# A Fourier mixing layer with a low-rank token mixer: where V, W1, W2 and the second batch are loaded

## The chip, the cores and the metric

The kernel runs on one core of a Trainium2 chip. The core has a matrix engine (TensorE, PE in the profile), a vector engine (VectorE, DVE), an activation engine (ScalarE, ACT), a general engine (GpSimd, POOL) and a queue engine that only issues transfers (SyncE, SP). Each engine works through its own instructions in order and waits for the others by semaphores. Transfers between the chip's memory and the on-chip buffers run on 16 DMA engines; they can be issued from SP (queue q1 in the profile), from ACT (q10) and from POOL (q0). The metric is the device time of one execution in microseconds (us); less is better. The time before is the median of three runs.

## The reference

The input `x` has 8 batches of 3136 tokens with 256 channels. A two-dimensional Fourier transform is taken over tokens and channels and its real part kept. To that a low-rank mixing of tokens is added, and then a channel MLP with a residual.

```python
X = np.fft.fft(np.fft.fft(x, axis=1), axis=2).real      # (8, 3136, 256)
h = X.transpose(0, 2, 1) @ U @ V                        # U (3136, 32), V (32, 3136)
u = X + h.transpose(0, 2, 1)
out = u + np.maximum(u @ w_ch1, 0.0) @ w_ch2            # (256, 1024), (1024, 256)
```

All arrays are float32.

## The kernel before

**Factoring of the transform.** 3136 is 49 times 64. Stage 1 transforms over one factor (`s1_single` for one batch, `s1_steps` for a pair), writes the result `z` to memory (`zturn`), and the *turn* (`turn`, L228) reads it back transposed as the coefficient tile `g`: 64 partitions, 25 blocks `k`, 256 channels, in runs of 512 bytes. Stage 3 (`s3_steps`, matmuls at L283) multiplies `g` with the table `T` and gives the tokens `q`. The lower half of `g`, partitions 64 to 127, holds the low-rank term: `te_single` (L256, one batch) or `te_steps` (L240, a pair) computes the projection of the signal on U; it is masked (`te_out`, L237) and copied into `g` 25 times (`spread`, L267). Half of `T` therefore holds V. The transform over channels is folded into the weights: stage 1's inputs are added and subtracted with their mirror images, and W1 is multiplied with a cosine and sine table `Q` before use (`W1p`, `W1m`). W2 is folded by an addition and a subtraction (`w2_fold`, L624).

**Order.** The order of instructions is written by hand. The *head* handles batch 0 alone, before any MLP work can start. In the code's order it issues the load of U on SP (L408) and batch 0's four x tiles on POOL (`load_single`, L107: a direct and a mirrored load each, cast from float32 to bf16), then on POOL V twice (L420 and L421, into partitions 64 to 95 and 96 to 127) and W1 (L423); builds tables on POOL, DVE and ACT; runs stage 1 in eight steps `s1b0[0]` to `s1b0[7]`, every second one storing to `zturn` (L222) from SP; and issues the turn (L569) on SP and ACT and W2's load (L572) on SP. POOL casts V into `T` (L582), ACT writes its mirrored part (L580), and after that come POOL's loads of batch 1 (L608, L609). TensorE then does `te_single` (L589), W1's product with `Q` (`w1ps`, L591 to L600, eight float32 matmuls) and the first stage-3 steps. `keep_warm(n)` (L437) issues n matmuls on zeros, so that TensorE isn't idle.

**The main loop.** For each pair of batches there are 13 chunks of up to 512 tokens, and for each chunk four steps: `mlp1` (L326) computes a quarter of the hidden layer of this chunk, `mlp2` (L338) a quarter of the outputs of the chunk before, which SP stores (L360, four stores every second step). `plan(p)` (L666) places all other work at these 52 steps of a pair: stage 3 of the current pair's second batch, and, by `place_next(nx, a, gap, s3lo)` (L675), the eight chunk loads of the next pair from step `a` on, `gap` steps apart, POOL's fold (L131) 3 steps behind each load, DVE's fold (L122 to L124) 6 behind, stage 1 (L172) 8 and 9 behind, the turn and the projection right after the last of them, and stage 3 from step `s3lo`. The pair 0 has batch 1 in addition: its stage 1 at steps 6 to 13, its turn at 15, `te_single` at 17, stage 3 at 20 to 31. Pair 1 is placed with `(9, 2.3, 43)`, pairs 2 and 3 with `(3, 2.3, 40)`. `load_uz` (L661, step 12) loads the projection's table `UZ` in two transfers of 1600 rows of 128 bytes.

Of the kernel before, what the change touches and what calls it, by code (L numbers as in the profile page):

```python
# [22 lines left out]
def kernel(  # L23
# [9 lines left out]
    nc = tc.nc  # L33
# [194 lines left out]
    def turn(pr, b, parts, engines=(nc.sync,)):  # L228
        g = gpool.tile([P, NK1, D], BF16, tag=f"g{b}", name="g")
        src = zd[pr.p % 2, b].rearrange("k cn d -> cn k d")  # L230
        for i, (k0, k1) in enumerate(parts):
            engines[i % len(engines)].dma_start(out=g[0:64, k0:k1], in_=src[:, k0:k1, :])
        pr.g[b] = g
# [22 lines left out]
    def te_single(pr, b, spread):  # L256

        ps = psd.tile([P, 2, D], FP32, tag="ps", name="teps")
        for k in range(NK1):
            nc.tensor.matmul(ps[0:64, 0, :], us[:, k], pr.g[b][0:64, k, :], start=(k == 0), stop=(k == NK1 - 1))  # L260
        te_out(pr, b, ps, slice(0, 64), spread)
# [153 lines left out]
    part[0][3] = load_single(0, 3)  # L415
    nc.gpsimd.memset(x32[0][:].bitcast(FP32), 0.0)
    part[0][0] = load_single(0, 0)
    kio_t = gpool.tile([P, NK1, D], BF16, tag="g0", name="kio")
    kio = kio_t[0:64].bitcast(I32).rearrange("p k (s j) -> p (k s) j", s=2)[:, 0:NK1, :]
    nc.gpsimd.dma_start(out=uv[64:96], in_=moe_V)  # L420
    nc.gpsimd.dma_start(out=uv[96:128], in_=moe_V)  # L421
    w1r = tmp([P, 2, H], "w1r", FP32R)
    nc.gpsimd.dma_start(out=w1r[:], in_=moe_w_ch1.rearrange("(h p) j -> p h j", p=P))  # L423

    nc.gpsimd.iota(kio, pattern=[[1, NK1], [N1, 64]], base=0, channel_multiplier=0)
    nc.gpsimd.iota(kio[32:33, 0:NK1:2], pattern=[[0, 13], [1, 64]], base=0, channel_multiplier=0)
# [8 lines left out]
    nc.vector.memset(idle.bitcast(FP32), 0.0)  # L435

    def keep_warm(n):  # L437
        ps = psh.tile([P, 2, 512], FP32, tag="h", name="warm")
        for i in range(n):
            nc.tensor.matmul(ps[:, 0], idle[:, 0:P], idle[:, P:640], start=True, stop=True)  # L440

    keep_warm(12)
    nc.vector.memset(pi[:], math.pi * (1.0 - 2.0 ** -21))
# [54 lines left out]
    ups_v = ups[0:64, :, 0:384].rearrange("p i (k r) -> p i k r", k=12)  # L498
    nc.scalar.copy(rv[:, :, :, 0, :], ups_v)
    ua = tmp([64, NK1, 64], "ua", FP16)  # L500
    A, V = copy_act, copy_dve
    s1b0 = list(s1_single(first, 0, part[0], [A, V, A, V, A, V, A, A],
                          lambda n: (nc.sync, nc.scalar if n == 7 else nc.sync)))
# [11 lines left out]
        ts(pv[:, 7 + i:8 + i], m[:], off, 192.0)  # L515
    s1b0[2]()
    s1b0[3]()
    keep_warm(3)
    for i in range(2):
        for t in range(3):  # L520
            ts(an2[:, i, t, :, i], jf[0:PR, 0:32], pv[:, 5 + i:6 + i], pv[:, 7 + t:8 + t])
    mask_bits(an2[:], 16)
    s1b0[4]()
    sin_of(Fs[:, 3:9], an2[:].rearrange("p a t k c -> p (a t) k c"), 16)
    s1b0[5]()


    pn = tmp([64, 2], "pn")
# [3 lines left out]
    nc.vector.memset(pn[32:33, 0:1], 0.5)  # L532
    nc.vector.memset(pn[32:33, 1:2], 32.25)
    ta2 = kio.bitcast(FP32)
    ts(ta2, kio, pn[:, 0:1], pn[:, 1:2])
    mask_bits(ta2, 18)

    for k0, k1 in [(0, 16), (16, 25)]:
        ps = psh.tile([P, 16, 64], FP32, tag="h", name="uups")
        for k in range(k0, k1):  # L540
            o = ps[0:64, k - k0]
            nc.tensor.matmul(o, ua[:, k], ub[:, k].unsqueeze(1).to_broadcast([64, 2, R]),
                             start=((k - k0) % 8 == 0), stop=True, skip_group_check=True)
            if k:
                mk = 24 - k
                nc.tensor.matmul(o, ua[:, k], rv[:, mk // 12, mk % 12].rearrange("p s r -> p (s r)"),
                                 start=False, stop=True, skip_group_check=True)
        (copy_dve if k0 else copy_act)(us[:, k0:k1], ps[0:64, 0:k1 - k0])
    keep_warm(2)
    s1b0[6]()  # L550
    s1b0[7]()
    sin_of(T[0:64, :, 0:64], ta2, 18)
    keep_warm(10)

    pl = tmp([P, 1], "pl")
    ts(pl[:], pf[:], 1.0 / D, None)
    jq = ypool.tile([P, 3, P], FP32, tag="y", name="jq")  # L560
    ts(jq[:, 0, 0:65], jf[:, 0:130:2], pl[:], 128.25)
    ts(jq[:, 0, 65:P], jf[:, 2:P:2], pl[:], 128.5)
    for i in range(2):
        ts(jq[:, 1 + i, 0:64], jf[:, 1:P:2], pl[:], 128.25 + 0.5 * i)
        ts(jq[:, 1 + i, 64:P], jf[:, 1:P:2], pl[:], 128.5 + 0.5 * i)
    mask_bits(jq[:], 16)
    Q = tmp([P, 3, P], "Q", FP32R)
    sin_of(Q[:], jq[:], 16)
    turn(first, 0, [(0, 8), (8, 16), (16, NK1)], [nc.sync, nc.scalar])  # L569
    g1 = gpool.tile([P, NK1, D], BF16, tag="g1", name="w2_f")  # L570
    w2_f = g1[:, 0:16].bitcast(FP32).rearrange("p (t s) d -> p t s d", s=2)
    nc.sync.dma_start(out=w2_f, in_=moe_w_ch2.rearrange("(t p) (s d) -> p t s d", p=P, s=2))  # L572
    nc.vector.tensor_copy(T[0:64, :, 64:128], T[0:64, :, 63::-1])
    sgv = tmp([P, 1], "sgv")
    ts(sgv[:], pf[:], 96.0, -2.0, AL.is_ge, AL.mult)
    ts(sgv[:], sgv[:], 1.0, None, AL.add)
    bp_sin = residual_tables()

    Vk = uv.rearrange("p (k2 k1) -> p k1 k2", k1=N1)
    nc.scalar.mul(T[64:128, 1:NK1, 64:128], Vk[64:128, 48:24:-1, :], sgv[64:128])  # L580
    for lo, hi in [(0, 9), (9, 17), (17, NK1)]:
        nc.gpsimd.tensor_copy(T[64:128, lo:hi, 0:64], Vk[64:128, lo:hi, :])  # L582
    held = []

    def spread_first(g, te):
# [5 lines left out]
    for c in range(2):  # L591
        cs = slice(c * 512, (c + 1) * 512)
        ps = psh.tile([P, 2, 512], FP32, tag="h", name="w1ps")
        for blk in range(2):
            for i in range(2):
                nc.tensor.matmul(ps[:, blk], Q[:, blk * (1 + i)], w1r[:, i, cs], start=(i == 0), stop=(i == 1))
        if c:
# [156 lines left out]
```

## Time and profile before

| What | us |
|---|---|
| median of three runs | 504.78 (502.74 to 511.37) |
| profiled execution, its own time | 506.79 |
| span of the profiled execution | 504.9 |
| first matmul on the first coefficients (L283) | 48.92 |
| first second-layer matmul (L345) | 58.65 |
| end of TensorE's work | about 496 |
| mean granted TensorE clock | 0.955 of full speed |

The span is the time between the first and the last instruction; the profiled execution took 1.9 us more than it, and 2.0 us more than the median. The page gives busy time and share of each engine, the span in 40 slices, the DMA queues, the chain of work that ended last, and the costliest groups of instructions. In the answers of the trace a row of a timeline gives the start, the duration, the engine, the source line, the operation with output and inputs, the shapes, the count, and in brackets how long the engine had been idle and what ended that. A row of a window gives each engine's busy time in it, then TensorE's granted clock, the busy share of the 16 DMA engines and the GB/s moved.

### The profile page before, as it was taken

Reading aid. Unit: us, or ns where it says so; the run is one execution under the profiler, and the core shown is the slowest. Engines: PE = TensorE matmul, PEld = TensorE weight load, DVE = VectorE, ACT = ScalarE, POOL = GpSimd, SP = SyncE. Lnnn points to the kernel's source line nnn. Section 1 sums busy time; section 2 is a strip of 40 time slices with the busy share of each in tenths; the row PEclk is TensorE's granted clock in tenths of the full one; section 3 lists DMA queues with packets and bytes.
Section 4 is the critical chain, followed back from the end, with each engine's and each line's share of the span. In section 5 each row is a group of like instructions: output and inputs, shape, how many; then the busy total and the mean of one; then the engine's idle time right before and its main releaser. Section 6 shows DMA issues by size and latency. Waiting matters only on the chain.

```text
span 504.9 us, 9394 instructions
## 1 busy us (share of the span) xinstructions
PE 446.6 (88%) x3624; PEld 319.3 (63%) x3684; DVE 221.3 (44%) x512; ACT 285.5 (57%) x387; POOL 138.8 (27%) x145
## 2 busy tenths in 40 slices
PE   6607899379999999998999999979999999999993
PEld 2405566256778677765777777756776777766772
DVE  7821642225752544757314535865225444221211
ACT  4421744316774655775655566768456655666660
POOL 7480032427513202655150005663130000000000
PEclk9965999859999999998999999999999999999998
DMA  9999047845747824885495226766582222222323
GB/s 131 199 164 176 3 116 211 207 98 169 212 132 163 181 64 133 223 261 167 133 160 169 50 69 194 227 215 187 139 153 60 64 65 69 68 74 69 89 53 75
DMA packets 69345, 68.03 MB, mean 135 GB/s; under 512 B 17412, under 2 KB 62284, under 8 KB 69236
## 3 DMA queue, kind: packets, MB, share of 16 engines
q1 hardware_dynamic: 53780, 44.93, 36.5%
q0 software_dynamic: 11536, 14.77, 14.3%
q10 hardware_dynamic: 3984, 7.73, 4.6%
q8 instruction: 29, 0.48, 0.4%
q14 instruction: 16, 0.13, 0.1%
HBM read 36.36 MB, written 34.28 MB: 140 GB/s over the span
## 4 chain that ended last, share of the span: by engine, by line
PE 71%; DVE 3%; DMA 3%; ACT 2%; issue 1%; SPq 1%; ACTq 0%; DVEq 0%
PE ops L345 30%; PE hps L334 28%; PE ops L348 4%; PE ps L283 3%; PE ps L172 2%; PE teps L248 2%; ACT hT L336 2%; DMA out_dram<-ob 2%; DMA g<-zturn 2%; DVE yb L124 1%; PE teps L260 1%; SPq L360 1%; DVE ob L355 1%; ACT om L354 1%; DVE yb L123 1%
## 5 line engine op out<-in xcount | busy, mean ns | idle before, releaser
L336 ACT ACTIVATE hT<-hps 128x1024 bf16<-128x1024 f32 (+1 forms) x208 | 202.4, 975 | 135.1 <-PE hps L334 121.9
L345 PE MATMUL ops<-W_91,hT 128*128 128x256 bf16 x1568 | 226.4, 274 | 0.5 <-DVE W_91 L625 0.3
L345 PEld LDWEIGHTS <-hT 128*128 128x128 bf16 x1568 | 146.0, 98 | 35.0 <-issue 0.3
L355 DVE TENSOR_TENSOR ob<-ops,om 128x256 f32<-128x256 f32 (+1 forms) x100 | 41.9, 419 | 203.3 <-ACT om L354 199.5
L334 PE MATMUL hps<-q,W1p 128*128 128x512 bf16 (+1 forms) x420 | 102.6, 355 | 3.3 <-DVE q L79 1.2
L334 PE MATMUL hps<-q,W1m 128*128 128x512 bf16 x354 | 96.9, 383 | 3.7 <-ACT hT L336 1.9
L131 POOL TENSOR_TENSOR y<-xa,xb 98x1020 f32<-98x1020 f32 (+1 forms) x24 | 55.0, 2293 | 125.8 <-DMA xa<-in_x_dram 95.9
L79 DVE CAST q<-ps 128x512 bf16<-128x512 f32 (+3 forms) x120 | 64.5, 559 | 25.5 <-PE ps L283 19.0
L334 PEld LDWEIGHTS <-W1p 128*128 128x128 bf16 x448 | 40.6, 98 | 28.3 <-issue 3.9
L76 ACT CAST z<-ps 128x512 bf16<-128x512 f32 x57 | 33.4, 586 | 39.2 <-PE ps L172 31.1
L334 PEld LDWEIGHTS <-W1m 128*128 128x128 bf16 x384 | 36.2, 99 | 29.2 <-issue 4.3
L348 PEld LDWEIGHTS <-q 128*128 128x128 bf16 x392 | 38.6, 98 | 21.6 <-issue 1.2
L354 ACT COPY om<-ops 128x256 f32<-128x256 f32 (+1 forms) x100 | 36.8, 368 | 9.9 <-PE ops L345 9.2
L356 DVE TENSOR_TENSOR ob<-ops,om 128x256 f32<-128x256 f32 (+1 forms) x100 | 40.9, 409 | 0.0
L283 PE MATMUL ps<-T,g 128*128 128x128 bf16 (+1 forms) x400 | 37.5, 219 | 1.5 <-DVE q L79 1.5
L348 PE MATMUL ops<-Bp,q 128*128 128x128 f16 x200 | 38.4, 219 | 0.0
L267 POOL COPY g<-te 64x1024 int32<-64x1024 int32 (+1 forms) x21 | 22.5, 1118 | 57.3 <-DVE te L237 31.8
L348 PE MATMUL ops<-Bm,q 128*128 128x128 f16 x192 | 37.3, 221 | 0.0
L260 PE MATMUL teps<-g,us 64*64 64x256 bf16 x50 | 11.0, 415 | 27.4 <-DMA g<-zturn 27.4
L283 PEld LDWEIGHTS <-g 128*128 128x128 bf16 x400 | 29.8, 99 | 6.8 <-issue 1.9
L102 POOL DMA_INDIRECT xb<-in_x_dram,idx x24 | 25.3, 1054 | 9.8 <-PE ps L216 5.2
L260 PEld LDWEIGHTS <-us 64*64 64x64 bf16 x50 | 8.3, 167 | 30.0 <-DMA g<-zturn 16.7
(129 smaller groups left out, 247.5 us busy)
## 6 DMA issues: line engine op xcount, KB each, us to landing
out_dram<-ob SPq DMA_DIRECT2D x392, 64.0 KB
xa<-in_x_dram SPq DMA_DIRECT2D x24, 392.0 KB
g<-zturn SPq DMA_DIRECT2D x7, 800.0 KB
zturn<-z ACTq DMA_DIRECT2D x9, 512.0 KB
xs<-in_x_dram POOLq DMA_DIRECT2D x16, 196.0 KB, 8.4
zturn<-z ACTq DMA_DIRECT2D x3, 448.0 KB
zturn<-z ACTq DMA_DIRECT2D x9, 128.0 KB
w1r<-in_moe_w_ch_dram POOLq DMA_DIRECT2D x1, 1024.0 KB, 15.0
```

Of the source, the lines that this page charges most:

```text
L76: nc.scalar.copy(o, i)
L79: nc.vector.tensor_copy(o, i)
L102: nc.gpsimd.indirect_dma_start(out=ck.xb.rearrange("p l d -> p (l d)"), out_offset=None, in_=x_g, in_offset=bass.IndirectOffsetOnAxis(ap=i ...
L131: nc.gpsimd.tensor_tensor(ck.y[:, 0:n, 1:256], ck.xa[:, 0:n, 1:256], rb[:, :, 255:0:-1], op=AL.add)
L283: nc.tensor.matmul(o, lt, r, start=st, stop=True, skip_group_check=True)
L334: nc.tensor.matmul(ps[:, i, 0:n], (W1p if ch.sg > 0 else W1m)[:, blk, j], q[:, blk, c0:c0 + n], start=(blk == 0), stop=(blk == 1))
L336: nc.scalar.activation(ch.h[:, 2 * jp:2 * jp + 2, 0:n], ps[:, :, 0:n], AF.Relu)
L345: nc.tensor.matmul(ps, ch.h[:, j, t * P:(t + 1) * P], W2[:, j, :], start=(j == 0 and t % 2 == 0), stop=(j == JT - 1), skip_group_check=True)
L348: nc.tensor.matmul(ps[:, j], q[:, j, tk], (Bp if ch.sg > 0 else Bm)[:, j], start=False, stop=False, skip_group_check=True)
L354: nc.scalar.copy(om[:, 0:n], ch.po[:, 0:n, 1])
L355: nc.vector.tensor_tensor(ob[:, 0:n, 0:P], ch.po[:, 0:n, 0], om[:, 0:n], op=AL.add)
L356: nc.vector.tensor_tensor(ob[:, 0:n, P:D], ch.po[:, 0:n, 0], om[:, 0:n], op=AL.subtract)
```

## The change

V is loaded once, on SP right after U. POOL casts it into `T` before its table work, and DVE copies the partitions 64 to 95 of `T` into 96 to 127. W1 is loaded on SP after the fourth stage-1 step; DVE adds and subtracts its halves, and `w1ps` becomes four matmuls. `w1ps` goes ahead of `te_single`, with eight warm matmuls before and after it. W2's load waits for batch 0's turn: a small copy on POOL reads all three parts of `g` and writes into W2's tile. The loads of batch 1, later on POOL, stand behind that copy. In the plan the stages have one more step between load and fold, and the placements of pair 0 and `place_next` get other numbers.

```diff
     nc.sync.dma_start(out=U_f, in_=moe_U.rearrange("(k2 k1) r -> k2 (k1 r)", k1=N1))
+    nc.sync.dma_start(out=uv[64:96], in_=moe_V)
...
-    kio_t = gpool.tile([P, NK1, D], BF16, tag="g0", name="kio")
...
-    nc.gpsimd.dma_start(out=uv[64:96], in_=moe_V)
-    nc.gpsimd.dma_start(out=uv[96:128], in_=moe_V)
-    w1r = tmp([P, 2, H], "w1r", FP32R)
-    nc.gpsimd.dma_start(out=w1r[:], in_=moe_w_ch1.rearrange("(h p) j -> p h j", p=P))
+    Vk = uv.rearrange("p (k2 k1) -> p k1 k2", k1=N1)
+    for lo, hi in [(0, 9), (9, 17), (17, NK1)]:
+        nc.gpsimd.tensor_copy(T[64:96, lo:hi, 0:64], Vk[64:96, lo:hi, :])
+    kio = UZ[0:64].rearrange("p a b -> p (a b)").bitcast(I32)[:, 0:64 * NK1].rearrange("p (k j) -> p k j", j=64)
...
-        ps = psh.tile([P, 2, 512], FP32, tag="h", name="warm")
+        ps = pso.tile([P, 2, 2, P], FP32, tag="o", name="warm")
...
     ua = tmp([64, NK1, 64], "ua", FP16)
+    nc.scalar.copy(T[64:96, 1:NK1, 64:128], Vk[64:96, 48:24:-1, :])
+    pl = tmp([P, 1], "pl")
+    ts(pl[:], pf[:], 1.0 / D, None)
+    jq = ypool.tile([P, 2, P], FP32, tag="y", name="jq")
...
+    w1_f = tmp([P, 2, H], "w1_f")
...
     s1b0[2]()
     s1b0[3]()
-    keep_warm(3)
+    nc.sync.dma_start(out=w1_f[:], in_=moe_w_ch1.rearrange("(h p) j -> p h j", p=P))
+    keep_warm(4)
...
     mask_bits(an2[:], 16)
-    s1b0[4]()
+    Q = tmp([P, 2, P], "Q", FP32R)
+    sin_of(Q[:], jq[:], 16)
     sin_of(Fs[:, 3:9], an2[:].rearrange("p a t k c -> p (a t) k c"), 16)
-    s1b0[5]()
...
     ta2 = kio.bitcast(FP32)
+    s1b0[4]()
+    s1b0[5]()
...
-        (copy_dve if k0 else copy_act)(us[:, k0:k1], ps[0:64, 0:k1 - k0])
-    keep_warm(2)
+        if k0:
+            copy_dve(us[:, k0:k1], ps[0:64, 0:k1 - k0])
+        else:
+            ups0 = ps
     s1b0[6]()
     s1b0[7]()
+    copy_act(us[:, 0:16], ups0[0:64])
+    nc.vector.tensor_copy(T[96:128, :, 0:64], T[64:96, :, 0:64])
+    ts(T[96:128, 1:NK1, 64:128], T[64:96, 1:NK1, 64:128], -1.0, None)
+    w1s = tmp([P, 2, H], "w1s", FP32R)
+    nc.vector.tensor_tensor(w1s[:, 0], w1_f[:, 0], w1_f[:, 1], op=AL.add)
+    nc.vector.tensor_tensor(w1s[:, 1], w1_f[:, 0], w1_f[:, 1], op=AL.subtract)
+    turn(first, 0, [(0, 8), (8, 16), (16, NK1)], [nc.sync, nc.scalar])
     sin_of(T[0:64, :, 0:64], ta2, 18)
-    keep_warm(10)
...
-    turn(first, 0, [(0, 8), (8, 16), (16, NK1)], [nc.sync, nc.scalar])
-    g1 = gpool.tile([P, NK1, D], BF16, tag="g1", name="w2_f")
-    w2_f = g1[:, 0:16].bitcast(FP32).rearrange("p (t s) d -> p t s d", s=2)
-    nc.sync.dma_start(out=w2_f, in_=moe_w_ch2.rearrange("(t p) (s d) -> p t s d", p=P, s=2))
     nc.vector.tensor_copy(T[0:64, :, 64:128], T[0:64, :, 63::-1])
...
-    nc.scalar.mul(T[64:128, 1:NK1, 64:128], Vk[64:128, 48:24:-1, :], sgv[64:128])
-    for lo, hi in [(0, 9), (9, 17), (17, NK1)]:
-        nc.gpsimd.tensor_copy(T[64:128, lo:hi, 0:64], Vk[64:128, lo:hi, :])
...
-    te_single(first, 0, spread_first)
+    keep_warm(8)
...
-            for i in range(2):
-                nc.tensor.matmul(ps[:, blk], Q[:, blk * (1 + i)], w1r[:, i, cs], start=(i == 0), stop=(i == 1))
+            nc.tensor.matmul(ps[:, blk], Q[:, blk], w1s[:, blk, cs], start=True, stop=True)
         if c:
-            held.append(lambda ps=ps, cs=cs: ts(W1p[:, :, cs], ps[:], 0.5, None))
+            ts(W1p[:, :, cs], ps[:], 0.5, None)
...
+    keep_warm(8)
+    bp_sin = residual_tables()
+
+    g1 = gpool.tile([P, NK1, D], BF16, tag="g1", name="w2_f")
+    w2_f = g1[:, 0:16].bitcast(FP32).rearrange("p (t s) d -> p t s d", s=2)
+    nc.gpsimd.tensor_copy(w2_f[0:64, 0, 0, 0:3], first.g[0][0:64, 7:NK1:8, 0])
+    nc.sync.dma_start(out=w2_f, in_=moe_w_ch2.rearrange("(t p) (s d) -> p t s d", p=P, s=2))
...
+    te_single(first, 0, spread_first)
...
-                for o, f in [(0, load), (3, fn), (6, fd), (8, s1[2 * c]), (9, s1[2 * c + 1])]:
+                for o, f in [(0, load), (4, fn), (7, fd), (9, s1[2 * c]), (10, s1[2 * c + 1])]:
                     at[int(a + gap * c) + o].append(f)
-            e = int(a + gap * 7) + 10
+            e = int(a + gap * 7) + 11
...
-            place([lambda: w2_fold(0), lambda: w2_fold(1)], 1, 3)
+            place([lambda: w2_fold(0), lambda: w2_fold(1)], 2, 4)
...
-            place(s1_single(cur, 1, part[1], [copy_act, copy_dve] * 4, lambda n: (nc.scalar, nc.scalar)), 6, 14)
-            place([lambda: turn(cur, 1, whole)], 15, 16)
-            place([lambda: te_single(cur, 1, spread_pool)], 17, 18)
+            place(s1_single(cur, 1, part[1], [copy_act, copy_dve] * 4, lambda n: (nc.scalar, nc.scalar)), 5, 13)
+            place([lambda: turn(cur, 1, whole)], 13, 14)
+            place([lambda: te_single(cur, 1, spread_pool)], 18, 19)
             place(s3_steps(cur, 1, copy_dve), 20, 32)
-            place_next(pairs[1], 9, 2.3, 43)
+            place_next(pairs[1], 12, 2.5, 43)
...
-                place_next(pairs[p + 1], 3, 2.3, 40)
+                place_next(pairs[p + 1], 0, 3.4, 40)
```

More of the change, by code (lines that the diff above doesn't have):

```diff
@@ L417 @@
     part[0][0] = load_single(0, 0)
-    kio_t = gpool.tile([P, NK1, D], BF16, tag="g0", name="kio")
-    kio = kio_t[0:64].bitcast(I32).rearrange("p k (s j) -> p (k s) j", s=2)[:, 0:NK1, :]
-    nc.gpsimd.dma_start(out=uv[64:96], in_=moe_V)
-    nc.gpsimd.dma_start(out=uv[96:128], in_=moe_V)
-    w1r = tmp([P, 2, H], "w1r", FP32R)
-    nc.gpsimd.dma_start(out=w1r[:], in_=moe_w_ch1.rearrange("(h p) j -> p h j", p=P))
+    Vk = uv.rearrange("p (k2 k1) -> p k1 k2", k1=N1)
+    for lo, hi in [(0, 9), (9, 17), (17, NK1)]:
+        nc.gpsimd.tensor_copy(T[64:96, lo:hi, 0:64], Vk[64:96, lo:hi, :])
+    kio = UZ[0:64].rearrange("p a b -> p (a b)").bitcast(I32)[:, 0:64 * NK1].rearrange("p (k j) -> p k j", j=64)
     nc.gpsimd.iota(kio, pattern=[[1, NK1], [N1, 64]], base=0, channel_multiplier=0)
@@ L437, in keep_warm @@
     def keep_warm(n):
-        ps = psh.tile([P, 2, 512], FP32, tag="h", name="warm")
+        ps = pso.tile([P, 2, 2, P], FP32, tag="o", name="warm")
         for i in range(n):
-            nc.tensor.matmul(ps[:, 0], idle[:, 0:P], idle[:, P:640], start=True, stop=True)
+            nc.tensor.matmul(ps[:].rearrange("p a s d -> p (a s d)"), idle[:, 0:P], idle[:, P:640], start=True, stop=True)
     keep_warm(12)
@@ L500 @@
     ua = tmp([64, NK1, 64], "ua", FP16)
+    nc.scalar.copy(T[64:96, 1:NK1, 64:128], Vk[64:96, 48:24:-1, :])
+    pl = tmp([P, 1], "pl")
+    ts(pl[:], pf[:], 1.0 / D, None)
+    jq = ypool.tile([P, 2, P], FP32, tag="y", name="jq")
+    ts(jq[:, 0, 0:65], jf[:, 0:130:2], pl[:], 128.25)
+    ts(jq[:, 0, 65:P], jf[:, 2:P:2], pl[:], 128.5)
+    ts(jq[:, 1, 0:64], jf[:, 1:P:2], pl[:], 128.25)
+    ts(jq[:, 1, 64:P], jf[:, 1:P:2], pl[:], 128.5)
+    mask_bits(jq[:], 16)
+    w1_f = tmp([P, 2, H], "w1_f")
     A, V = copy_act, copy_dve
@@ L547 @@
                                  start=False, stop=True, skip_group_check=True)
-        (copy_dve if k0 else copy_act)(us[:, k0:k1], ps[0:64, 0:k1 - k0])
-    keep_warm(2)
+        if k0:
+            copy_dve(us[:, k0:k1], ps[0:64, 0:k1 - k0])
+        else:
+            ups0 = ps
     s1b0[6]()
     s1b0[7]()
-    sin_of(T[0:64, :, 0:64], ta2, 18)
-    keep_warm(10)
[L558 to L561, printed above, removed]
@@ L562 @@
-    ts(jq[:, 0, 65:P], jf[:, 2:P:2], pl[:], 128.5)
-    for i in range(2):
[L564 to L568, printed above, removed]
-    turn(first, 0, [(0, 8), (8, 16), (16, NK1)], [nc.sync, nc.scalar])
+    copy_act(us[:, 0:16], ups0[0:64])
+    nc.vector.tensor_copy(T[96:128, :, 0:64], T[64:96, :, 0:64])
+    ts(T[96:128, 1:NK1, 64:128], T[64:96, 1:NK1, 64:128], -1.0, None)
@@ new lines @@
+    w1s = tmp([P, 2, H], "w1s", FP32R)
+    nc.vector.tensor_tensor(w1s[:, 0], w1_f[:, 0], w1_f[:, 1], op=AL.add)
+    nc.vector.tensor_tensor(w1s[:, 1], w1_f[:, 0], w1_f[:, 1], op=AL.subtract)
+    turn(first, 0, [(0, 8), (8, 16), (16, NK1)], [nc.sync, nc.scalar])
+    sin_of(T[0:64, :, 0:64], ta2, 18)
+    nc.vector.tensor_copy(T[0:64, :, 64:128], T[0:64, :, 63::-1])
+    keep_warm(8)
+    for c in range(2):
+        cs = slice(c * 512, (c + 1) * 512)
+        ps = psh.tile([P, 2, 512], FP32, tag="h", name="w1ps")
+        for blk in range(2):
+            nc.tensor.matmul(ps[:, blk], Q[:, blk], w1s[:, blk, cs], start=True, stop=True)
+        if c:
+            ts(W1p[:, :, cs], ps[:], 0.5, None)
+        else:
+            nc.scalar.mul(W1p[:, :, cs], ps[:], 0.5)
@@ L570 @@
+    keep_warm(8)
+    bp_sin = residual_tables()
     g1 = gpool.tile([P, NK1, D], BF16, tag="g1", name="w2_f")
     w2_f = g1[:, 0:16].bitcast(FP32).rearrange("p (t s) d -> p t s d", s=2)
+    nc.gpsimd.tensor_copy(w2_f[0:64, 0, 0, 0:3], first.g[0][0:64, 7:NK1:8, 0])
     nc.sync.dma_start(out=w2_f, in_=moe_w_ch2.rearrange("(t p) (s d) -> p t s d", p=P, s=2))
-    nc.vector.tensor_copy(T[0:64, :, 64:128], T[0:64, :, 63::-1])
-    sgv = tmp([P, 1], "sgv")
-    ts(sgv[:], pf[:], 96.0, -2.0, AL.is_ge, AL.mult)
@@ L576 @@
-    ts(sgv[:], sgv[:], 1.0, None, AL.add)
-    bp_sin = residual_tables()
-    Vk = uv.rearrange("p (k2 k1) -> p k1 k2", k1=N1)
-    nc.scalar.mul(T[64:128, 1:NK1, 64:128], Vk[64:128, 48:24:-1, :], sgv[64:128])
-    for lo, hi in [(0, 9), (9, 17), (17, NK1)]:
-        nc.gpsimd.tensor_copy(T[64:128, lo:hi, 0:64], Vk[64:128, lo:hi, :])
     held = []
@@ L589 @@
     te_single(first, 0, spread_first)
[L591 to L597, printed above, removed]
-            held.append(lambda ps=ps, cs=cs: ts(W1p[:, :, cs], ps[:], 0.5, None))
-        else:
-            nc.scalar.mul(W1p[:, :, cs], ps[:], 0.5)
     s3b0 = list(s3_steps(first, 0, copy_alt))
@@ L603 @@
         s()
-    held[1]()
     held[0]()
```

## The prediction

> **What bounds the kernel now.** I read the engine totals and the chain of waits on the page first, then TensorE's waits, then the places of those waits in the timelines, then clock and DMA traffic in short windows.
>
> ```profile
> PE 446.6 (88%) x3624; PEld 319.3 (63%) x3684; DVE 221.3 (44%) x512; ACT 285.5 (57%) x387; POOL 138.8 (27%) x145
> ...
> PE 71%; DVE 3%; DMA 3%; ACT 2%; issue 1%; SPq 1%; ACTq 0%; DVEq 0%
> ```
>
> TensorE bounds: no other engine passes 57%. So only two things shorten the span: less TensorE idle time (504.9 - 446.6 = 58 us) and less time at half clock. The change removes almost no matmul work. Where the idle time lies (us in total, times, longest):
>
> ```profile
> PE teps L260 <- DMA g<-zturn: 27.4, 2, 16.2
> PE ps L172 <- DVE yb L124: 5.3, 2, 2.8
> ```
>
> Two waits of batches 0 and 1 for the turned coefficients `g` make 27.4 us, two waits for DVE's folds in later pairs 5.3. The rest is mainly the start (about 10) and the drain after 496 (9), which stay. Timelines of TensorE and of SP's queue:
>
> ```profile
> 39.87 5.54 PE L260 MATMUL teps<-g,us 64*64 64x256 bf16 x25 [16.22 <-DMA g<-zturn]
> 45.34 3.78 PE L596 MATMUL w1ps<-w1r,Q 128*128 128x512 f32 x8
> 48.92 0.86 PE L283 MATMUL ps<-T,g 128*128 128x64 bf16 x8
> ...
> 104.07 5.49 PE L260 MATMUL teps<-g,us 64*64 64x256 bf16 x25 [11.18 <-DMA g<-zturn]
> ...
> 29.39 1.27 SPq L232 DMA_DIRECT2D g<-zturn  x2
> ...
> 87.94 5.25 SPq L360 DMA_DIRECT2D out_dram<-ob  x4
> ...
> 96.36 0.65 SPq L232 DMA_DIRECT2D g<-zturn  x1
> ...
> 156.99 1.60 SPq L232 DMA_DIRECT2D g<-zturn  x2
> ```
>
> The first turn is issued at 29.39, lands at 39.87 (10.5 us), and TensorE then does te (5.5) and w1ps (3.8) before the first coefficient matmul at 48.92. Clock (the number before the DMA share) in windows over these waits:
>
> ```profile
> 23.50:29.00 5.50, 0.15 (x1) 0.00 (x0) 4.28 (x15) 1.44 (x2) 4.72 (x6) 1.00 0.79 263
> 29.00:39.50 10.50, 0.00 (x0) 0.00 (x0) 0.08 (x1) 3.00 (x1) 7.57 (x11) 0.50 1.09 148
> 39.50:49.50 10.00, 9.63 (x40) 7.22 (x41) 1.11 (x2) 1.02 (x1) 0.00 (x0) 0.50 1.15 187
> ...
> 104.00:114.00 10.00, 9.71 (x43) 6.62 (x44) 3.60 (x4) 1.61 (x2) 3.86 (x3) 0.50 0.19 63
> ```
>
> Each long wait halves the clock for 10 us of work behind it, some 5 us lost a time. DMA queues in 36 to 38 and, last row, in 161 to 163:
>
> ```profile
> q1 hardware_dynamic: 365, 0.18, 60.0%
> q10 hardware_dynamic: 253, 0.13, 41.3%
> q0 software_dynamic: 290, 0.05, 31.1%
> ...
> q1 hardware_dynamic: 702, 0.35, 120.3%
> ```
>
> The first turn moved 618 packets in 2 us beside batch 1's loads (q0); a turn alone moves 702.
>
> **The change: the head.** *Turn issue.* It waits for the last `zturn` store. One of two 392 KB loads of V goes. DMA was busy without a pause from 2 to 27.6 at some 180 GB/s, so that is worth 0.4 MB, about 2 us. V now runs before x's loads instead of behind them: the x tiles come up to 2 us later (part 0 from 18.9, its second load issued at 7.96 plus 10.9 to landing, to about 20.5), the stores with them. W1's issue on SP (1.54, W2's row) falls near 16.5, after part 2's stores and clear of part 3's near 20; POOL is rid of three issues (1.8). Then 400 waiting store packets (1.1 us at the 390 a us that 62% of 240 in 27:28 implies), W1 (1 MB at the 334 GB/s of 24 to 26: 3.1), the rest of the stores (1.3) and the 1 us from last packet to issue: about 27.5, 1.9 earlier.
> Here a rule speaks against the change. Between 18 and 20 POOL's queue took 93% and SP's, with the stores, 15%: stores were starved behind V and W1. The Trainium skill, "DMA: Bandwidth & Descriptors", section "Queues, rings and completion order", says that an engine takes turns between queues packet by packet, but works one ring in order. So W1 on SP stands wholly ahead of the stores of parts 3 and 0, which on POOL's queue could pass it: up to 3.1 us later, an issue near 30.6. By the trace W1's bytes go through before the last stores either way (last POOL-queue packet 27, last store 28.6), so I take 27.5 and keep 30.6 for the range.
> *Landing.* With W2 and batch 1 held back the turn runs alone. 1600 packets at 351 a us are 4.6, plus about 2 before the first packet and 0.7 after the last (156.99 to 164 for the pair's first half): 7.3 for 10.5. Landed at 34.8.
> *Behind it.* w1ps is moved ahead of te and half its matmuls go: off the path 3.8. Its cover is the wait: W1 lands about 25.5, DVE's add and subtract are two at 1.22 (row of W2's fold), so w1ps runs at 28 and the second 8 warm matmuls end near 31. If that cover is gone (W1 at 31 or later) te starts late by the excess. te's result now goes to `g` in the open: +1.3 (DVE 0.42 and 0.69, and passing).
> *Clock.* Gaps are 23.4 to 28 and 31 to 34.8, both shorter than the 5.4 (23.65 to 29.1) and 4.4 (92.9 to 97.3) that the clock held. The skill's "TensorE: Matmul & The Clock Gate", section "HAM oscillation — how this bites in real kernels", allows no gap above about 3.4 us: by it both are at risk, and te costs 5.5 instead of 2.8. By the trace: 34.8 + 2.8 + 1.3 = 38.9 for the first coefficient matmul; by the rule 41.6; before 48.92.
> *W2.* This is what is late next. POOL's small copy waits for the turn, and SP's W2 and POOL's eight batch-1 loads (5.9 us of issue from 28.08) stand behind it. SP has nothing else due. W2 issues at 35.2 (1.54), moves from 37 beside q0; before it took 38 to 48 in part beside the turn: landed 46 to 47.5. DVE reaches the fold at 44.5, waits, and two folds of 1.22 end near 49.5; the first mlp2 would be ready at 48.3. So first mlp2 about 49.8 against 58.65: **-8.8**. The W2 wait also hides the clock's choice. Ends -5 (W1 ahead in the ring) and -10.5 (no W2 wait). Batch 1's first part lands by 43 and is used at 51 or later: nothing.
> *At nothing.* POOL's T casts (3.59) go from 24 to 9, where POOL then has its x issues done; ACT's V copy (3.00) fills its idle 8 to 10.8; jq's operations (1.2) stand before DVE's first idle of 1.61; T's copies to 96:128 (two, 1.4 and 1) end before W1 lands. All are covered by the DMA-bound x loads; without cover at most about 2.
> **Second turn.** Issued two steps earlier and te one step later. But SP's issue at 96.36 stood behind step 15's stores, delayed by `UZ`'s load (4.30) and the slowed stores after it (5.25 for the usual 2.4). `UZ` stays at step 12, so the new turn stands behind those: about 93.5 on the old clock, 3 earlier, landing at 100.8. te moves from 92.9 to 94.6. Wait about 6.2 for 11.2: **-5**. Ends 0 and, were SP free by 90, -8 with a warm clock 4.7 more. At 6.2 the clock falls.
> **Pair 1's coefficients.** Its eight chunk loads start at step 12, 2.5 apart: last stage-1 step at 39 (34 before), turn at 40, first use still at 43. From the end of that step to the turn's issue took 6.2 (150.8 to 156.99), landing 7.0: 13.2. TensorE has in between steps 40 to 43: four mlp1 of 0.9, one mlp2 of 1.1, te 3.5: 8.0. New wait of 5.2, and half a chance of the half clock (up to 4.5). I take **+6**, ends +3 and +10. POOL's spread (two times 4 us, te ends 7.2 in) is ready at about 12, under it.
> **Pairs 2 and 3.** Loads 3.4 apart instead of 2.3, folds one step later in reach. The waits of 2.5 and 2.8 lie at 229.6 and 338, in a stretch of 230 and 237 GB/s where stores and loads crowd; a third fewer bytes a us should remove them, with 0.6 beside: **-5.5**, ends -3 and -6.5. Their turn goes to step 34, use at 40: TensorE has about 13.9 for the 13.2 needed, so 0.
> **Sum.** -8.8 - 5 + 6 - 5.5 = -13.3. The profiled execution took 506.79 (span 504.9 and 1.9 around it), 2 above the median 504.78 of the runs: 493.5 against it, **491.5** against the median.
>
> **The rivals.**
> *SP gets free early* (for: two x loads fewer at steps 9 and 11; against: `UZ`'s 3,200 small packets remain). The second wait drops near 3, the clock stays up: -3 and -4.7, 484.
> *New waits eat more* (for: step 43's margin is plainly negative): the clock falls there (+4) and W1 delays the stores (+3): 498.5.
> *Slower: all three pairs' turns late.* The margin is -5.2 at step 43, about +0.7 at step 40 of pairs 2 and 3. If store-to-landing takes d longer than 13.2, each pair loses about d and the clock, 4.5 a time: 3d + 11 in all. Past the slower bound (514.9) from d near 4. At d = 6, 521. Against it: after step 26 only the output stores share the queues, and 156.99 to 164 shows such a turn.
> *It doesn't do what it says*: W1 in the ring and W2's late fold return the head's gain down to -3, 497; it joins the second.
>
> **How the numbers follow.** As worked 0.50 (487 to 496), SP early 0.20, eaten 0.23, slower 0.07. The range 482 to 501 leaves out the slower case and a little at both sides. The measurement tells about 2% from no change, that is below 494.7 or above 514.9: most of the first case and all of the second are faster, 0.62; within 0.31; slower 0.07.
>
> **What would show it.** First te at 34 to 36 with clock 1.00; DVE waiting for W2 near 45; a g wait before the second te of 3 to 7; a new TensorE wait for `g` at L283 near 150; no wait for yb L124. Wrong if te comes after 38, if L283 waits in pairs 2 and 3, or if the second te's wait stays above 9.

## The result and the profile after

The changed kernel takes 490.18 us in the median (489.2 to 493.19, four runs) against 505.73 for the kernel before on the same chip; the ratio is 0.9722 with a 95% interval of 0.9649 to 0.9795, that is about 14 us. The ratio leaves out one slow execution of the kernel before (511.37). The forecast was 491.5. The profiled executions differ by more, 17.6 us: 506.79 before, 489.20 after (spans 504.9 and 487.4).

The totals of the page after, and its chain by engine:

```profile
PE 451.9 (93%) x3685; PEld 317.9 (65%) x3685; DVE 223.6 (46%) x512; ACT 286.1 (59%) x387; POOL 138.2 (28%) x143
...
PE 72%; DVE 10%; DMA 8%; SPq 3%; ACT 3%; issue 2%; ACTq 0%; POOL 0%; DVEq 0%; POOLq 0%
```

TensorE still bounds. Its busy total reads 5 us higher than before, but the two totals don't compare: 60 matmul records are missing in the trace before (3624 matmuls beside 3684 weight loads; none is missing after), so some of the 58 us of idle time before was work. The waits compare better: those that the trace lists for TensorE add up to 46.4 us before and 26.8 after. The largest ones after, with the folds' (us in total, times, longest):

```profile
PE teps L260 <- DMA g<-zturn: 6.2, 1, 6.2
PE ps L283 <- DMA g<-zturn: 4.5, 1, 4.5
PE ps L172 <- DVE q L79: 2.4, 5, 0.8
PE w1ps L586 <- DVE w1s L575: 2.2, 1, 2.2
...
PE ps L172 <- DVE yb L124: 0.2, 1, 0.2
```

Of two waits for `g` at te one is left, with 6.2 us. The first has gone altogether. A new one stands at L283, and the waits for DVE's folds have fallen from 5.3 to 0.2. The timelines of SP and TensorE at the same places as before:

```profile
24.00 1.27 SPq L232 DMA_DIRECT2D g<-zturn  x2
...
26.11 3.11 PE L440 MATMUL warm<-W1m 128*128 128x512 bf16 x8
29.15 2.91 PE L260 MATMUL teps<-g,us 64*64 64x256 bf16 x25
33.37 0.57 PE L283 MATMUL ps<-T,g 128*128 128x64 bf16 x8 [1.31 <-DVE g L267]
...
44.22 0.27 PE L345 MATMUL ops<-W_91,hT 128*128 128x256 bf16 x1 [1.13 <-DVE W_91 L628]
...
87.69 5.49 PE L260 MATMUL teps<-g,us 64*64 64x256 bf16 x25 [6.22 <-DMA g<-zturn]
...
150.94 0.55 PE L283 MATMUL ps<-T,g 128*128 128x64 bf16 x8 [4.51 <-DMA g<-zturn]
```

The turn is issued 5.4 us earlier, the first te takes 2.91 instead of 5.54, and the first second-layer matmul stands at 44.22 instead of 58.65. POOL's small copy, which needs the whole turn, starts at 30.65, so the turn landed by then, 6.6 after its issue. The first te, which reads the turn's three parts in order of `k`, begins at 29.15, before the last part is needed, and does not wait. From milestone to milestone (first matmul of each kind, us):

| Milestone | before | after | difference | gained or lost since the last |
|---|---|---|---|---|
| first second-layer matmul | 58.65 | 44.22 | -14.4 | -14.4 |
| pair 1's first stage 3 (step 43) | 165.65 | 150.94 | -14.7 | -4.8, and a new wait of +4.5 |
| pair 1's second batch (step 3 of the next pair) | 190.57 | 177.53 | -13.0 | +1.7 |
| end of the span | 504.9 | 487.4 | -17.5 | -4.5 |

Each column of this table is one execution. How much the head varies from one to the next is told with the first two experiments.

### The profile page after: what moved, and what is told of

The parts are those of the page before. It is cut to its first block, busy times and chain, and to the rows that moved or that the text cites. A ratio compares the mean times of both kernels' runs of the same rounds, so it can differ in the third digit from the quotient of the medians.

```text
span 487.4 us, 9451 instructions
## 1 busy us (share of the span) xinstructions
PE 451.9 (93%) x3685; PEld 317.9 (65%) x3685; DVE 223.6 (46%) x512; ACT 286.1 (59%) x387; POOL 138.2 (28%) x143
## 4 chain that ended last, share of the span: by engine, by line
PE 72%; DVE 10%; DMA 8%; SPq 3%; ACT 3%; issue 2%; ACTq 0%; POOL 0%; DVEq 0%; POOLq 0%
PE hps L334 29%; PE ops L345 28%; PE ps L283 4%; PE ops L348 4%; DMA g<-zturn 3%; DMA out_dram<-ob 3%; SPq L360 2%; PE ps L172 2%; ACT hT L336 2%; DVE q L79 2%; PE teps L260 2%; DMA xs<-in_x_dram 2%; PE teps L248 1%; DVE yb L122 1%; DVE ob L356 1%
## 5 line engine op out<-in xcount | busy, mean ns | idle before, releaser
L334 PE MATMUL hps<-q,W1p 128*128 128x512 bf16 (+1 forms) x448 | 107.0, 362 | 2.4 <-DVE q L79 1.8
L334 PE MATMUL hps<-q,W1m 128*128 128x512 bf16 x384 | 100.0, 384 | 0.2 <-ACT hT L336 0.2
L283 PE MATMUL ps<-T,g 128*128 128x128 bf16 (+1 forms) x400 | 37.5, 219 | 7.2 <-DMA g<-zturn 4.5
L76 ACT CAST z<-ps 128x512 bf16<-128x512 f32 x57 | 33.5, 588 | 13.1 <-PE ps L172 10.9
L283 PEld LDWEIGHTS <-g 128*128 128x128 bf16 x400 | 29.6, 98 | 13.1 <-POOL g L267 5.0
L102 POOL DMA_INDIRECT xb<-in_x_dram,idx x24 | 25.4, 1059 | 10.9 <-PE ps L216 6.0
L122 DVE TENSOR_TENSOR yb<-y 98x508 bf16<-98x508 f32 (+1 forms) x24 | 27.2, 1134 | 0.8 <-POOL y L131 0.8
L172 PE MATMUL ps<-yb,F 98*128 98x258 bf16 (+1 forms) x108 | 18.9, 265 | 2.6 <-DVE q L79 2.4
```

The costliest lines, as they stand in the source:

```text
L76: nc.scalar.copy(o, i)
L122: nc.vector.tensor_tensor(o[:, :, 1:128], i[:, :, 1:128], i[:, :, 255:128:-1], op=AL.add)
L283: nc.tensor.matmul(o, lt, r, start=st, stop=True, skip_group_check=True)
L334: nc.tensor.matmul(ps[:, i, 0:n], (W1p if ch.sg > 0 else W1m)[:, blk, j], q[:, blk, c0:c0 + n], start=(blk == 0), stop=(blk == 1))
```

## The experiments

All ratios are to the kernel before, run on the same chip beside the experiment. The theory was: the head and the plan are two gains that add; the head gains because the turn is issued earlier and runs alone; the second te hangs on SP's queue, pair 1's new wait on a lack of two steps; the folds' waits went with the spacing of the loads.

**The head alone.** The plan's old numbers put back into the changed kernel, `w2_fold` excepted:

```diff
-place_next(pairs[1], 12, 2.5, 43)
+place_next(pairs[1], 9, 2.3, 43)
-place_next(pairs[p + 1], 0, 3.4, 40)
+place_next(pairs[p + 1], 3, 2.3, 40)
```

with the distances 3, 6, 8, 9, batch 1's stage 1 at 6, its turn at 15 and te at 17.

> The changed kernel with the plan's old numbers (w2_fold keeps its new place). Theory (the head and the plan add up, and the head is the large part): first mlp2 stays near 44.2, the second te waits 10 to 11 us again and two waits for yb L124 come back, pair 1's L283 doesn't wait; 490 to 494 us. Rival (the head's gain is lost at the second turn, because that turn hangs on SP's queue and not on TensorE): second te starts near its old 104, 500 us or more. Rival (the plan carries the gain): 500 or more with the second te early.

Measured: 493.81 us, ratio 0.9763 (0.9724 to 0.9802). TensorE's waits:

```profile
PE teps L260 <- DMA g<-zturn: 10.2, 1, 10.2
PE ps L172 <- DVE yb L124: 4.3, 2, 2.3
```

The waits are as the theory had them: the second wait of 10.2 is back, and so are two waits for yb; L283 doesn't wait. Both rivals fall: the second te starts at 91.19, and the time is well below 500. The first second-layer matmul came at 46.42, though, not near 44.2, with the same code ahead of it. In the ten profiles with this head unedited it stands between 43.70 and 47.20.

**The plan alone.** The kernel before with the plan's new numbers, `w2_fold` excepted.

> The kernel before with the plan's new numbers alone (w2_fold stays). Theory (additive): the head as before (first mlp2 58.65), second te waits about 6 instead of 11, pair 1's L283 waits about 4.5, no wait for yb L124; 501 to 505 us, that is 1 to 5 below before. Rival (the plan carries the gain): 495 or less. Rival (without the shorter head the plan's new wait outweighs it): 506 or more.

Measured: 500.09 us, ratio 0.9885 (0.9838 to 0.9931), just below the range. The second te waits 5.5, L283 4.2, yb not at all. SP's and TensorE's timelines:

```profile
27.61 1.27 SPq L232 DMA_DIRECT2D g<-zturn  x2
...
32.70 1.91 PE L260 MATMUL teps<-g,us 64*64 64x256 bf16 x8 [11.45 <-DMA g<-zturn]
...
38.31 2.08 PE L260 MATMUL teps<-g,us 64*64 64x256 bf16 x9 [1.46 <-DMA g<-zturn]
...
53.06 0.27 PE L345 MATMUL ops<-W,hT 128*128 128x256 bf16 x1 [0.32 <-DVE W L625]
```

The head was expected as before, with the first second-layer matmul at 58.65. It came at 53.06, with the code of the kernel before ahead of it: the turn was issued 1.8 us earlier, and its first part was there when te could begin with it, 7.2 us sooner. What made the difference is not shown; it is one of two profiles of the old head. So a single profile before and one after do not give the head's worth, and the ratios are the better measure: the head alone is worth about 12 us (10 to 14), the plan alone about 6 (3.5 to 8). The product of the two ratios is 0.9651, at the lower edge of the changed kernel's interval: the two add, within what this can tell. The head is the larger part.

**Holding back W2 and batch 1.** The copy on POOL gets another source, which is ready at 22:

```diff
-nc.gpsimd.tensor_copy(w2_f[0:64, 0, 0, 0:3], first.g[0][0:64, 7:NK1:8, 0])
+nc.gpsimd.tensor_copy(w2_f[0:64, 0, 0, 0:3], us[:, 0:3, 0])
```

> The changed kernel, but POOL's small copy reads us (ready near 22) instead of g, so W2 and batch 1 are loaded beside the turn as before. Theory (a turn alone lands sooner): turn issued at 24, landing 9.5 to 10.5 us later instead of 6.6, first L283 near 36.5 to 37.5, no wait for W2; 491 to 493.5. Rival (holding back only moves the transfers behind the turn, where W2 is waited for): 488 to 490.5. Third: POOL's loads also delay the last zturn stores, turn issued at 26 or later, 494 or more.

Measured: 497.6 us, ratio 0.9826 (0.9779 to 0.9872). The time is that of the third case, its mechanism isn't: the turn goes out at 23.61, as early as before the edit. SP's and TensorE's timelines:

```profile
23.61 1.27 SPq L232 DMA_DIRECT2D g<-zturn  x2
...
34.47 5.77 PE L260 MATMUL teps<-g,us 64*64 64x256 bf16 x25 [5.45 <-DMA g<-zturn]
41.55 0.93 PE L283 MATMUL ps<-T,g 128*128 128x64 bf16 x8 [1.31 <-DVE g L267]
```

te starts 10.9 us after the issue. The clock falls during the wait of 5.45, so te takes 5.77. The first stage 3 comes at 41.55 instead of 33.37: 5.3 us for the later start and 2.9 for the slower te. The clock stays at 0.50 until 49.3. That the turn lands sooner alone is shown. The expectation put its worth at 1 to 3 us, where the times give 7, mainly because it left out the clock.

**W1's queue.** W1's load moved from SP to POOL, behind the x tiles:

```diff
+w1_f = tmp([P, 2, H], "w1_f")
+nc.gpsimd.dma_start(out=w1_f[:], in_=moe_w_ch1.rearrange("(h p) j -> p h j", p=P))
...
-nc.sync.dma_start(out=w1_f[:], in_=moe_w_ch1.rearrange("(h p) j -> p h j", p=P))
```

> The changed kernel with W1 loaded from POOL right behind the x tiles instead of from SP. Theory (what counts are the bytes ahead of the last stores, not the queue they are in): turn issued between 23.5 and 25, 488.5 to 491. Rival by ring order (on SP W1 stands in front of the last stores, on POOL they pass it): turn at 22 or earlier, 486 to 488. Rival by starvation (W1's large packets on POOL's queue take turns with every small packet of the stores, as in the kernel before): turn at 26 or later, 491.5 to 494.

Measured: 489.72 us, ratio 0.9654 (0.9605 to 0.9704). SP's timeline:

```profile
22.69 1.27 SPq L232 DMA_DIRECT2D g<-zturn  x2
```

In the ten profiles with the unedited head the issue lies between 23.5 and 26.5, so this one is 0.8 us ahead of the earliest. It lies between the theory's range, 23.5 to 25, and that of the rival by ring order, 22 or earlier; the rival by starvation falls. The time can't be told from that of the changed kernel. So W1's place on SP, which the title of the change names, is worth nothing that these runs can tell. Its folding on DVE, and V's single load, were not tried alone.

**UZ behind the second turn.** `load_uz` at step 18 instead of 12.

```diff
-place([load_uz], 12, 13)
+place([load_uz], 18, 19)
```

> The changed kernel with load_uz at step 18 instead of 12, so that its two transfers are no longer ahead of batch 1's turn on SP. Theory (the second turn hangs on SP's queue behind UZ): turn issued 2 to 4 us earlier against step 13, second te waits 2 to 4 instead of 6.2, and if the clock stays up another 4 are won: 482 to 487. Rival (the turn hangs on the zturn stores or on step 13's output stores): issue and wait unchanged within 1 us, 488.5 to 490.5.

Measured: 486.74 us, ratio 0.9639 (0.9555 to 0.9723). The second turn in the changed kernel (first row), and with this edit the turn and te:

```profile
80.09 0.65 SPq L232 DMA_DIRECT2D g<-zturn  x1
...
77.56 0.62 SPq L232 DMA_DIRECT2D g<-zturn  x1
...
85.26 5.49 PE L260 MATMUL teps<-g,us 64*64 64x256 bf16 x25 [3.20 <-DMA g<-zturn]
```

The first second-layer matmul stands at 44.22 and 46.45, so the turn is issued 31.1 us after it instead of 35.9, and te waits 3.20 instead of 6.22. So `UZ` did hold it up, for about half of the wait. The clock fell all the same and te took 5.49. On its time alone this kernel can't be told from the changed one.

**The second te later.** te at step 20, batch 1's stage 3 at 22 to 29.

```diff
-place([lambda: te_single(cur, 1, spread_pool)], 18, 19)
-place(s3_steps(cur, 1, copy_dve), 20, 32)
+place([lambda: te_single(cur, 1, spread_pool)], 20, 21)
+place(s3_steps(cur, 1, copy_dve), 22, 30)
```

> The changed kernel with the second te at step 20 instead of 18 and batch 1's stage 3 in steps 22 to 29 instead of 20 to 31. Theory (the wait of 6.2 and the half clock behind it cost what the trace shows): two steps of 2 us cover 4, the wait falls to 1 to 3, the clock stays at 1.00: 480 to 485. Rival (the wait returns as another one: stage 3 packed into fewer steps makes TensorE wait for DVE's copies): 487 to 490.

Measured: 491.12 us, ratio 0.9714 (0.9649 to 0.978). The theory's 480 to 485 was missed. The rival's mechanism came true, at a time 1 us above its range. TensorE's waits:

```profile
PE ps L172 <- DVE q L79: 7.2, 6, 3.5
PE ps L283 <- DMA g<-zturn: 4.3, 1, 4.3
PE teps L260 <- DMA g<-zturn: 3.1, 1, 3.1
```

The wait for te halves as planned, but te still runs at half clock (5.49), and with stage 3 in fewer steps TensorE waits for DVE's copies, 3.5 at once.

**Pair 1 two steps earlier.** Its first load goes to step 10.

```diff
-place_next(pairs[1], 12, 2.5, 43)
+place_next(pairs[1], 10, 2.5, 43)
```

> The changed kernel with pair 1's loads from step 10 instead of 12. Theory (the wait of 4.5 for g at L283 is a lack of two steps between the turn and step 43): the wait falls to 0.5 or less, 484.5 to 486.5. Rival (two steps earlier the loads stand ahead of batch 1's turn on SP and in the DMA queues and lengthen the second te's wait by as much): 488.5 to 490.5.

Measured: 485.55 us, ratio 0.9619 (0.9552 to 0.9686). TensorE's timeline:

```profile
87.71 5.49 PE L260 MATMUL teps<-g,us 64*64 64x256 bf16 x25 [7.49 <-DMA g<-zturn]
...
149.08 0.55 PE L283 MATMUL ps<-T,g 128*128 128x64 bf16 x8 [0.94 <-DMA g<-zturn]
```

L283 waits 0.94 instead of 4.51, a little more than the theory's 0.5. The second te waits 7.49 instead of 6.22, so a part of the rival holds too. The interval of the ratio overlaps with that of the changed kernel.

**The spacing of pairs 2 and 3.** The old spacing, all else as changed.

```diff
-place_next(pairs[p + 1], 0, 3.4, 40)
+place_next(pairs[p + 1], 3, 2.3, 40)
```

> The changed kernel with the loads of pairs 2 and 3 placed as before (from step 3, 2.3 apart), the step more between load and fold kept. Theory (the spacing takes the waits for yb L124 away): they come back at two places, 2 to 3 us each, 493 to 495. Rival (the added step between load and fold is what took them away): 489 to 490.5.

Measured: 488.11 us, ratio 0.9646 (0.9571 to 0.972), and TensorE does not wait for yb at all. The theory fell. That led to the reverse:

**The distances of before.** The spacing 3.4 stays, folds and stage 1 stand 3, 6, 8 and 9 steps behind the load again.

```diff
-for o, f in [(0, load), (4, fn), (7, fd), (9, s1[2 * c]), (10, s1[2 * c + 1])]:
+for o, f in [(0, load), (3, fn), (6, fd), (8, s1[2 * c]), (9, s1[2 * c + 1])]:
...
-e = int(a + gap * 7) + 11
+e = int(a + gap * 7) + 10
```

> The changed kernel with the new spacing of the loads kept, but with the distances of before between load, folds and stage 1 (3, 6, 8, 9 steps; turn at 10 behind the last load). Theory (the added step, and not the spacing, took the waits for yb L124 away): waits of stage 1 (L172) for yb come back in pairs 2 and 3, 2 to 3 us each, while pair 1's L283 waits less, since its turn comes a step earlier (2 to 3 instead of 4.5); 489 to 493. Rival (each of the two alone is enough): no such wait, 486 to 489.

Measured: 491.51 us, ratio 0.9695 (0.965 to 0.974). TensorE's waits:

```profile
PE teps L260 <- DMA g<-zturn: 6.1, 1, 6.1
PE ps L283 <- DMA g<-zturn: 4.6, 1, 4.6
PE ps L172 <- DVE yb L124: 4.4, 3, 1.7
```

The waits for yb are back, three of 1.0 to 1.7. With the old distances they come to 4.3 (old spacing, the head alone) and 4.4 (new spacing); with the new distances to nothing (old spacing) and 0.2 (new spacing). So it is the step between load and fold that took them away, and the spacing did nothing for them. The ratio does not show what the step is worth: it can't be told from that of the changed kernel. That pair 1's wait would shrink was wrong: it stayed at 4.6.

**Both repairs.** `load_uz` at 18 and pair 1 from step 10, the edits of the two experiments above together.

> The changed kernel with load_uz at step 18 and pair 1's loads from step 10, both at once. Theory (two separate waits, so their gains of about 3.4 and 4.6 add): second te waits 3 to 5, pair 1's L283 at most 1; 480.5 to 483.5. Rival (pair 1's earlier loads take the free place on SP ahead of the turn, so the gains don't add): 484.5 to 486.5.

Measured: 482.14 us, ratio 0.9512 (0.9436 to 0.9587), an interval wholly below that of the changed kernel. TensorE's timeline:

```profile
84.11 5.49 PE L260 MATMUL teps<-g,us 64*64 64x256 bf16 x25 [2.42 <-DMA g<-zturn]
```

The second te waits 2.42, less than the expected 3 to 5, but still runs at half clock. L283 waits at most 0.8. The gains add, within what the ratios can tell.

**Warm matmuls ahead of te**, on top of that:

```diff
+for i in range(warm):
+    nc.tensor.matmul(ps[:, 1, :], W1m[:, 0, 0:P], W1m[:, 0, 0:D], start=True, stop=True,
+                     skip_group_check=True)
 for k in range(NK1):
...
-place([lambda: te_single(cur, 1, spread_pool)], 18, 19)
+place([lambda: te_single(cur, 1, spread_pool, warm=32)], 18, 19)
```

> As j_uz_pair1, with 32 matmuls of 256 columns on W1m, written to the unused half of te's PSUM tile, ahead of the second te. Theory (a wait of 3 to 4 costs the clock as well, and TensorE's idling is what lowers it): clock 1.00 through the te, te takes 2.8 to 3 instead of 5.5, and the matmuls behind it run at full speed; 3.5 to 4.5 below j_uz_pair1. Rival (the small 64-row te lowers the clock by itself, or what is won is waited for again behind it): within 1 us of j_uz_pair1.

Measured: 482.09 us, ratio 0.952 (0.9477 to 0.9563). TensorE's timeline, then its waits:

```profile
80.99 3.66 PE L260 MATMUL teps<-W1m 128*128 128x256 bf16 x32
84.58 2.91 PE L263 MATMUL teps<-g,us 64*64 64x256 bf16 x25
```

```profile
PE ps L172 <- DVE q L79: 5.2, 4, 3.3
PE ps L286 <- DMA g<-zturn: 2.4, 1, 2.4
```

te runs at full clock, in 2.91, and batch 1's stage 3 begins at 91.36 instead of 95.66. Yet pair 1's stage 3 begins at 146.22 against 146.66. Between the two, TensorE waits 3.3 for DVE at once and 2.4 for `g`, 5.7 in all where the kernel without the warm matmuls waits 3.4 (waits above 0.3), and behind the wait for DVE, at 96.4, the clock falls for 3.4 us, half of which is lost. Together that is nearly all of the 4.3 us gained. The mechanism of the theory is shown, its gain is not; the second half of the rival holds.

**The turn at step 12**, with both repairs and 16 warm matmuls.

```diff
-place([lambda: turn(cur, 1, whole)], 13, 14)
+place([lambda: turn(cur, 1, whole)], 12, 13)
```

> As k_warm, with batch 1's turn at step 12 instead of 13 and 16 matmuls ahead of te. Theory (the turn stood behind step 13's output stores and x's load on SP): issued 1.5 to 3 earlier, te waits at most 2 with its 16 matmuls, 1 to 2.5 below k_warm. Rival (then it waits for the zturn stores, and the output stores behind it on SP hold up DVE and TensorE): the same as k_warm or slower.

Measured: 483.11 us, ratio 0.9581 (0.9533 to 0.963). TensorE's timeline:

```profile
92.01 0.57 PE L286 MATMUL ps<-T,g 128*128 128x64 bf16 x8 [3.98 <-POOL g L270]
```

The turn goes out at 72.39 instead of 76.89, earlier than expected, and te no longer waits, but stage 3 of batch 1 then waits 4.0 for POOL's copies of te's result. Its executions spread from 478.76 to 486.21, so no gain over the two kernels before it is shown.

The fastest versions measured are the two with ratios 0.951 and 0.952, about 2% below the changed kernel by their ratios.

## Why the prediction was right

The forecast of 491.5 stands 1.3 us from the median, and its change of -13.3 is near the 14 us that the ratio gives. By the milestones the four terms add up to -17.5 instead. A part of that is the choice of executions: the one profiled before was 2.0 us slower than its median, the one after 1.0 faster than its own. So it is luck in part that the forecast comes so near. Three of the four terms were right in size, one of them for a wrong reason, and the head was put too small.

*The head: -8.8 predicted, -14.4 measured by the milestones and about -12 (10 to 14) by the ratio of the head alone.* The milestones' figure is outside the ends that the prediction gave (-5 and -10.5). The direction and the parts hold; the term was mis-sized at its beginning, in the turn's issue. "The x tiles come up to 2 us later" was wrong. They came earlier: the last one landed at 17.0 (issued at 8.29, 8.7 to landing) instead of 18.9, and its matmuls began at 18.51 instead of 20.09. V's load ahead of them did not make them late, though POOL's packets start only at 5; why they were early is not shown. W1 and the stores behind it then did not have to wait. The working's own terms (1.1, 3.1, 1.3 and 1 ahead of 27.5) let their bytes begin near 21. SP's queue in 17 to 22 after:

```profile
q1 hardware_dynamic: 637, 1.39, 96.1%
```

That is 1.39 MB in 5 us, 278 GB/s: slower than the 334 of the working, but begun some 4 us sooner, when POOL's queue was empty. So the turn went out at 24.0 instead of 27.5, and landed in 6.6 instead of 7.3. te began at 29.15, 1.5 before the last part had landed, where the working had it behind the whole turn; its sign "first te at 34 to 36" was missed to the early side. The feared delay by W1's place in the ring was not seen, and with W1 on POOL's queue the turn went out only 0.8 earlier than the earliest other, without a gain in time. W2, issued at 30.86, was in time: the 1.13 us at 44.22 are DVE's fold, which waited for nothing. The first te ran at full clock as predicted, but not for the reason given. The clock did fall, after gaps of 2.21 and 0.57, and rose again just before te, behind w1ps and the warm matmuls (the clock is the third number from the end):

```profile
25.00:26.00 1.00, 1.00 (x3) 0.50 (x3) 0.00 (x0) 1.00 (x1) 0.00 (x0) 0.57 0.53 161
26.00:28.00 2.00, 2.00 (x6) 0.78 (x6) 1.61 (x2) 1.27 (x2) 0.00 (x0) 0.50 1.20 204
28.00:29.00 1.00, 1.00 (x5) 0.25 (x2) 0.89 (x7) 0.00 (x0) 0.00 (x0) 0.72 1.20 177
29.00:32.00 3.00, 3.00 (x27) 2.60 (x25) 1.10 (x7) 0.00 (x0) 1.20 (x4) 1.00 0.18 28
```

On this point the Trainium skill's rule ("TensorE: Matmul & The Clock Gate", section "HAM oscillation — how this bites in real kernels", no gap above about 3.4 us) was nearer than my 5.4, but it is not safe here either: waits of 3.20, 3.09 and 2.42 ahead of the second te lost the clock in three of the experiments. In the changed kernel the clock fell once more in the head, at 35.4, after waits of only 1.31, 0.66 and 0.40. It was back at 38.8; the prediction had no term for that.

*The second turn: -5 predicted, -4.8 measured*, with the wait at 6.22 as worked out (6.2). That `UZ` on SP still held the turn up is shown by moving it, for about half of the wait.

*Pair 1's coefficients: +6 predicted, +6.2 measured.* The wait is 4.51 for 5.2. The clock, which was given half a chance, fell for 3.4 us (151.4 to 154.8), which fits the 1.7 lost behind the wait. Loads two steps earlier take the wait away, as the working implied.

*Pairs 2 and 3: -5.5 predicted, -4.5 measured.* The size was right by luck, since the cause was wrong: not fewer bytes a us, but the step more between load and fold took the waits for yb away.

The rivals: SP did not get free early by itself. The change did what it says, but of its title's parts the held-back transfers are shown to carry 5 us of the head by the ratios (0.9826 less 0.9722, of 505.73) and 7 by the times, and W1's queue nothing that can be told; for V and the folds on DVE it stays open. Pairs 2 and 3 never waited for their turns, so the slower case found no ground.

## What to carry to other kernels

Put a long transfer that nobody needs yet behind the one that everybody waits for, and count the clock with the wait: here a turn that landed 4 us sooner was worth 5 to 7 us. A plan written by hand should be checked at each place where distance from producer to consumer got shorter, by counting steps against the measured latency (13 us from the last stage-1 step to landed coefficients); that found the one new wait before it existed. When a change moves two knobs at once, undo each alone before naming the one that worked. And take the worth of a part from repeated runs: a single pair of profiles gave 14.4 us for the head, where the same old head varied by 5.6 between two profiles.

## What was not expected of the hardware

The small matmuls of te, 64 by 64 in the array, did not raise the clock. After the second wait TensorE was busy without a pause, yet the clock stayed low through all of te, 5.5 us, and rose only 3.6 us into the full-size matmuls that follow from 93.1 on:

```profile
88.00:93.00 5.00, 5.00 (x25) 3.84 (x23) 0.00 (x0) 0.00 (x0) 0.00 (x0) 0.50 0.73 239
93.00:96.00 3.00, 3.00 (x12) 1.55 (x12) 0.42 (x1) 0.96 (x1) 2.23 (x3) 0.50 0.00 0
96.00:98.00 2.00, 2.00 (x14) 1.26 (x13) 0.59 (x2) 0.60 (x3) 1.92 (x2) 0.80 0.03 8
```

In the head the clock was down for 3.4 us (25.1 to 28.6) while TensorE ran w1ps and the full-size warm matmuls without a pause. At full clock te kept it (29.15 to 32.1 in the head, and 84.58 to 87.5 with the warm matmuls ahead). So the 10 us of half clock that the kernel before pays at each wait are te's 5.5 and some 4 more.

Where one gap alone lost the clock, it fell between 1.8 us (54.0 to 55.9, a wait of 1.82) and 5.4 us after the gap's beginning in these traces. A part of that can be read off. Only 0.50 and 1.00 occur in these traces, so the mean of a window gives the instant of the change: 0.57 in 25 to 26 above puts the fall at 25.14, and 0.72 in 28 to 29 the rise at 28.56. More of them after:

```profile
35.00:36.00 1.00, 0.60 (x5) 0.24 (x4) 0.69 (x1) 0.98 (x2) 1.00 (x2) 0.69 0.91 223
38.00:39.00 1.00, 1.00 (x5) 0.38 (x4) 0.00 (x0) 0.58 (x1) 0.95 (x2) 0.60 1.29 174
...
55.00:56.00 1.00, 0.16 (x1) 0.10 (x1) 0.79 (x2) 0.00 (x0) 0.00 (x0) 0.93 0.77 184
59.00:60.00 1.00, 1.00 (x12) 0.61 (x11) 0.26 (x1) 0.27 (x1) 0.00 (x0) 0.86 0.27 67
...
86.00:87.00 1.00, 0.00 (x0) 0.00 (x0) 0.00 (x0) 0.00 (x0) 0.00 (x0) 0.79 1.06 221
```

These give 35.38, 38.80, 55.86, 59.28 and 86.58. All of these instants, and the rise at 96.8, lie a whole number of steps of 3.41 us after the first (1, 3, 4, 9, 10, 18 and 21 steps). So in this trace the clock changes only at points of a fixed grid: a short gap can lose it where a longer one elsewhere does not, and once lost it is gone for 3.41 us or a multiple of that. How much work a step must hold to keep the clock stays open.
